# Spreading the finish of the sixth and seventh attention batch over more places of the schedule, with the scatters five places later

## The chip, the cores and the metric

The kernel runs on one core of a Trainium2 chip. The metric is the time of one execution on the device in microseconds (us). The engines are TensorE (PE, with PEld its weight loads), VectorE (DVE), ScalarE (ACT), GpSimd (POOL) and SyncE (SP). SP only issues transfers here. POOL computes and also issues the indirect transfers (gathers and scatters) and the small reads of the routing table. Every engine works off its own list of instructions in order, so an instruction that waits holds up all that stand behind it on its engine.

## What is computed

Block-causal attention over 8 batches (8 heads, 576 positions, head size 64), whose output is the input of a mixture of 8 experts in which every token goes to one expert:

```python
scores = scale * np.matmul(q, k.transpose(0, 1, 3, 2))
scores = np.where(block_i >= block_j, scores, -1e9)     # blocks of 64
attn = softmax(scores); x = (attn @ v)                  # 4608 tokens x 512
logits = x @ w_gate
e_idx = np.argmax(logits, axis=1)                       # the token's expert
gate_w = softmax(logits)[token, e_idx]
eom = 1.0 / (1.0 + np.exp(-(x @ w_output_gate)))
for e in range(8):                                      # tokens of one expert
    h = np.maximum(x[mask] @ w1[e], 0.0)                # 512 -> 1024
    out[mask] = gate_w[mask] * eom[mask, e] * (h @ w2[e])
```

## The kernel before

**Attention runs in 34 positions.** Position p = 0 to 31 does the scores and the softmax of one pair of heads; four positions make a batch, numbered b = 0 to 7 (so batch 5 is the sixth and batch 6 the seventh). The pair's probabilities are transposed one position later and multiplied with v two positions later, so positions 32 and 33 only drain. The order inside a position is the list `PLAN`. Each `|` in it is a *round* (eight per position, r0 to r7), at which every running generator of the list `later` does one step:

```python
PLAN = """
    F0 S1 S0 M1 C0 | | E4- F1 C1 F2 M0 C2 Z0 E1A E1B E0A S2 E0B | F3 F4 C3 V0 Z1 S3 C4 |
    M2 F6 F5 E2A E2B M3 | C5 C6 V1 S4 VM | E3A E3B X M4 | | XM
"""
```

S, M and E are the scores of a row tile (PE), their maximum (DVE, L407 and L411) and the exponentials (ACT, L422); F and C are the transposes of the probabilities (PE, L456) and the copies out of PSUM (L1110); V, VM and X are the products with v. The instruction of L411 (`M4`, the maximum of the last row tile) comes once per position, late in it. It serves below as a clock: *the mark of position p*.

**The finish of a batch** (`finish_steps`) starts at r0 of position 4b+6: the logits of both gates (`logits`, L549), transposed and scaled (`turn_logits`, `scale_logits` L578, `scale_last` L590), summed over the heads (`heads`, L597 and L598), the choice of the expert (`choose`, L601 to L611), ranks in the expert (`ranks`, `own`, `slots`), the gate (`shares`, `gather`, `gate`, `weights`) and the scatter of five row tiles of (token, weight) into the table `tab_d` in DRAM (`scatter`, L658). `T(t)` transposes a row tile of x (PE, L561) and `K(t)` scales it and stores it to `x_d` (DVE, L566). A list with one entry per round says which step comes where. There are three such lists: *pace 1* with 32 entries, *pace 2* with 16 and *pace 3* with 12. Before the change batches 0 to 4 take pace 1, batches 5 and 6 pace 2, batch 7 pace 3. In pace 1 `heads` and two products of `choose` are POOL's, in pace 2 and 3 they are DVE's.

**Loading.** `load_heads` loads a *unit* of four heads (two positions), splits q and k into two fp16 parts on POOL (L105 and L108, eight pieces over eight rounds), turns each half by a DMA transpose (L112, on SP), and copies k's halves across (`swap`, `sw`, L117, DVE).

**The first expert.** `load_first` starts at r0 of position 28: `route_first` takes the counts of batches 0 to 5 (`run_cnt`, column 6) and picks the fullest expert, then its w1 and w2 are loaded. `fetch_ids` (L853) reads table rows, `fetch_x` (L864) gathers rows of x into `xg`; the first three tiles of it may only read the table after the scatters of batches 0 to 5. Eleven rounds later `split_slowly` splits w1 on POOL (L898 and L899, sixteen quarters, one per round, each behind an instruction of ACT), later POOL subtracts for w2 (L894, four chunks). PE needs the gathered x from position 33 on, w1 at the first L1024 (first layer of the experts) and w2 at the first L1053 (second layer).

**The seam.** After batch 7's finish `route_rest` makes a table of steps on DVE; then POOL reads more table rows, gathers x, SP loads the next weights, and the steady loop over the experts' steps begins (L1024 with `xt`, which a DMA transpose delivers).

On POOL, which no hand-written order covers, the scheduler places instructions by the program's order and its own estimate of readiness; on PE, DVE and ACT the written order holds from position 1 on.

Of the kernel before, what the change touches and what calls it, by code (L numbers as in the profile page):

```python
# [11 lines left out]
F32 = mybir.dt.float32  # L12
I32 = mybir.dt.int32
U32 = mybir.dt.uint32
AF = mybir.ActivationFunctionType
ALU = mybir.AluOpType
AX = mybir.AxisListType
PSUM = bass.MemoryType.PSUM
DRAM = bass.MemoryType.DRAM
IOA = bass.IndirectOffsetOnAxis  # L20

P = 128
# [5 lines left out]
def block_attention_top1_moe(  # L28
# [11 lines left out]
    nc = tc.nc  # L40
    B, H, S, D = q.shape
# [466 lines left out]
    def finish_batch(b, sums, xT, pace):  # L508

        for fns in finish_steps(b, sums, xT, pace):  # L510
            for fn in fns:
                fn()
            yield

    def finish_steps(b, sums, xT, pace):
# [13 lines left out]
        se = small.tile([P, NT], F32, name="se")  # L529
        sli = small.tile([P, NT], I32, name="sli")  # L530
        held = {}
        eng = nc.gpsimd if pace == 1 else nc.vector

        def bank():
            return ps_t.tile([P, 512], F32, name="ps_t")
# [90 lines left out]
        def own():  # L626
            nc.vector.tensor_tensor(rk, held["p"][:, 0:NT * E].rearrange("p (t e) -> p t e", e=E), oh, ALU.mult)

        def slots():
            rank = small.tile([P, NT], F32, name="rank")  # L630
            nc.vector.tensor_reduce(rank, rk, AX.X, ALU.add)
            add = small.tile([P, E], F32, name="add")
            nc.vector.tensor_reduce(add, oh.rearrange("p t e -> p e t"), AX.X, ALU.add)
            nc.vector.tensor_tensor(run_cnt[:, b + 1], run_cnt[:, b], add, ALU.add)
            sl = small.tile([P, NT], F32, name="sl")
            nc.vector.scalar_tensor_tensor(sl, er, -float(NTOK), rank, ALU.mult, ALU.add)
            nc.vector.tensor_scalar(sli, sl, float(E * NTOK), None, ALU.add)
# [16 lines left out]
        def scatter():  # L654
            for t in range(NT):
                r = ROWS[t]

                sc = nc.gpsimd.indirect_dma_start(  # L658
                    out=tab_d, out_offset=IOA(ap=sli[0:r, t:t + 1].bitcast(U32), axis=0),
                    in_=idg[0:r, b, t, :], in_offset=None,  # L660
                ).ins
                if scatters:
                    tc.declare_no_dep(sc, group="scatters", reason="distinct slots")
                for ins in tab_init + tab_reads:
                    tc.add_manual_dep(sc, ins.name, SYNC, reason="after earlier accesses of the table")
                tc.add_to_no_dep_group("scatters", sc)
                scatters.append(sc)
# [4 lines left out]
        if pace == 3:  # L672
            return [
                [lge], [ke, lgb], [kb, recips], [turn_logits, turn_last], [scale_logits, scale_last, heads, T(0)], [K(0), choose],
                [ranks], [own, T(1)], [slots, shares, K(1), T(2)], [gather, K(2), gate, T(3)], [weights, scatter, K(3), T(4)], [K(4)],
            ]
        if pace == 2:
            hooks["Z0"] = kb
            hooks["Z1"] = lambda: [fn() for fn in (turn_logits, scale_logits, turn_last, scale_last)]
            return [  # L680
                [lge, lgb], [ke], [recips], [], [heads, T(0)], [K(0), choose], [], [T(1)],
                [K(1), ranks], [own, T(2)], [K(2), slots, shares], [T(3), gather], [K(3), gate], [T(4), weights], [K(4), scatter], [],
            ]
        return [
            [lge], [ke, lgb], [kb, recips], [turn_logits], [scale_logits], [turn_last], [scale_last], [heads],
            [], [], [T(0)], [K(0)], [], [choose], [], [],
            [], [T(1), ranks], [own, K(1), T(2)], [K(2)], [T(3), slots], [shares], [K(3)], [],
            [], [], [T(4)], [K(4)], [gather], [gate], [weights, scatter], [],
        ]

    def counts(col, name):
# [231 lines left out]
    def load_first():  # L923

        route_first()
        fetch_ids(steps[0])
        fetch_ids(steps[1], (0, 1))
        fetch_x(steps[0])
        fetch_x(steps[1], (0, 1))
        with chain():  # L930
            ev = nc.sync.value_load(f_i[0:1, 0:1], min_val=0, max_val=E - 1)

        wc = {}

        def load(w, c):
            dt, nm = ((F16, "hh"), (BF16, "hl"))[c % 2]
            wc[c] = fs.tile([P, KF, 2, P], dt, name=nm).rearrange("p f h n -> p (f h n)").bitcast(F32)
            nc.sync.dma_start(quarter(w, wc[c]), rows_of(w, ev, c))

        for c in range(4):  # L940
            load(w1, c)
        for r in range(11):
            yield
        for c in range(4):
            yield from split_slowly(w1b[0][:, 0, c], w1b[0][:, 1, c].bitcast(BF16), wc[c].rearrange("p (g m) -> p g m", g=KF))
            load(w2, c)
        for r in range(5):
            yield
        for c in range(4):
            with tc.issue_after(last_act[0].ins):  # L950
                split_w2(nc.gpsimd, 0, wc[c], c)
            yield
# [150 lines left out]
    def advance(plan, p, parts, at=()):  # L1103
# [23 lines left out]
        if p > B * NP:  # L1127
            kept.pop("X-", lambda: None)()
        if done:
            later.append(finish_batch(*done, 1 if done[0] < B - 3 else 2 if done[0] < B - 1 else 3))  # L1130
        prods.extend(nxt)

    w1b, w2b, xg = [], [], []
# [163 lines left out]
```

## Time and profile before

| | |
|---|---|
| three timed runs, median | 763.81 us (761.55 to 764.34) |
| the profiled execution's own time | 760.33 us |
| its span, from the first to the last instruction | 758.4 us |
| PE busy | 724.5 us, 96% |
| DVE, ACT, POOL busy | 525.5, 532.1, 341.5 us |
| mark of position 31, the last one with scores | 347.14 us |
| first matmul of the experts' first layer | 360.06 us |

PE is busy almost everywhere, and the changed kernel has the same PE instructions, so what can change is the time in which PE waits or is held back. The granted TensorE clock is 0.998 over the span. Everything that the change moves lies between 100 and 410 us; from there on the loop over the experts is the same.

### The profile page before, as it was taken

Reading aid. Unit: us, or ns where it says so; the run is one execution under the profiler, and the core shown is the slowest. Engines: PE = TensorE matmul, PEld = TensorE weight load, DVE = VectorE, ACT = ScalarE, POOL = GpSimd, SP = SyncE. Lnnn points to the kernel's source line nnn. Section 1 sums busy time; section 2 is a strip of 40 time slices with the busy share of each in tenths; the row PEclk is TensorE's granted clock in tenths of the full one; section 3 lists DMA queues with packets and bytes.
Section 4 is the critical chain, followed back from the end, with each engine's and each line's share of the span. In section 5 each row is a group of like instructions: output and inputs, shape, how many; then the busy total and the mean of one; then the engine's idle time right before and its main releaser. Section 6 shows DMA issues by size and latency. Waiting matters only on the chain.

```text
span 758.4 us, 18741 instructions
## 1 busy us (share of the span) xinstructions
PE 724.5 (96%) x6918; PEld 510.5 (67%) x6918; DVE 525.5 (69%) x1058; ACT 532.1 (70%) x1193; POOL 341.5 (45%) x481
## 2 busy tenths in 40 slices
PE   5899999999999998889998999999999999999996
PEld 3677776767676665666866759667586676686662
DVE  6766776767776779676747958578587685895540
ACT  4999887988888886867117758577576675876531
POOL 6664647474757557396448423232222333301111
PEclk9999999999999999999999999999999999999999
DMA  8899877979696976862167997999999978741611
GB/s 153 175 207 189 178 168 151 203 131 218 123 217 105 214 151 138 198 183 78 64 222 214 290 308 198 290 272 377 294 299 328 302 208 287 222 78 43 240 41 45
DMA packets 256629, 147.87 MB, mean 195 GB/s; under 512 B 224144, under 2 KB 224208, under 8 KB 256528
## 3 DMA queue, kind: packets, MB, share of 16 engines
q1 hardware_dynamic: 248416, 127.30, 67.0%
q0 software_dynamic: 8112, 19.29, 7.8%
q8 instruction: 56, 0.92, 0.6%
q14 instruction: 45, 0.37, 0.2%
HBM read 126.03 MB, written 19.34 MB: 192 GB/s over the span
## 4 chain that ended last, share of the span: by engine, by line
PE 69%; DVE 10%; DMA 7%; ACT 7%; issue 4%; POOL 2%; POOLq 1%; SPq 0%; DVEq 0%; ACTq 0%
PE ps_s L1024 23%; PE ps_t L1053 19%; PE ps_t L456 7%; PE ps_a L491 5%; ACT pt L422 4%; DMA tr<-sp 4%; PE ps_s L390 3%; PE ps_s L391 3%; POOL tab_d L658 2%; PE ps_t L499 1%; PE ps_t L561 1%; ACT pT L1110 1%; DVE nmx L407 1%; PE ps_s L399 1%; PE ps_a L1077 1%
## 5 line engine op out<-in xcount | busy, mean ns | idle before, releaser
L1024 PEld LDWEIGHTS <-w1b 128*128 128x128 f16 (+1 forms) x2208 | 176.1, 98 | 26.1 <-DVE w1b L894 2.7
L1024 PE MATMUL ps_s<-xt,w1b 128*128 128x256 f16 (+5 forms) x1920 | 175.5, 253 | 3.2 <-DMA xt<-xr 1.8
L422 ACT ACTIVATE pt<-ps_s,nbs 128x512 f32<-128x512 f32 (+4 forms) x282 | 155.8, 577 | 25.5 <-DVE nbs L415 24.0
L1053 PE MATMUL ps_t<-w2b,hh 128*128 128x512 f16 (+1 forms) x560 | 166.9, 379 | 0.0
L894 DVE TENSOR_TENSOR w2b<-w2f,w2b 128x1024 bf16<-128x1024 f32 x80 | 92.9, 1220 | 88.8 <-ACT w2b L892 88.8
L407 DVE TENSOR_REDUCE nmx<-ps_s 128x2 f32<-128x1024 f32 (+1 forms) x125 | 102.6, 821 | 45.3 <-PE ps_s L392 44.3
L1110 ACT COPY pT<-ps_t 128x512 f32<-128x512 f32 (+1 forms) x221 | 112.7, 565 | 15.4 <-PE ps_t L456 15.2
L1062 POOL DMA_INDIRECT out_dram<-ys,ids x38 | 48.9, 1288 | 155.2 <-ACT ys L1061 87.7
L456 PE MATMUL ps_t<-ident,pt 128*128 128x128 f32 x768 | 108.5, 277 | 5.2 <-ACT pT L1110 2.9
L1053 PE MATMUL ps_t<-w2b,hl 128*128 128x512 f16 x280 | 106.2, 379 | 0.0
L1061 ACT ACTIVATE ys<-ps_t,ids 128x512 f32<-128x512 f32 (+1 forms) x38 | 26.1, 686 | 113.6 <-PE ps_t L1053 91.5
L1053 PEld LDWEIGHTS <-hh 128*128 128x128 f16 x560 | 54.3, 98 | 61.5 <-issue 0.3
L456 PEld LDWEIGHTS ps_t<-ident,pt 128*128 128x128 f32 x768 | 84.4, 141 | 15.4 <-ACT lgT L555 5.9
L894 DVE TENSOR_TENSOR w1b<-w1f,w1b 128x1024 bf16<-128x1024 f32 x80 | 92.9, 1217 | 1.0 <-ACT w1b L892 0.9
L108 POOL TENSOR_TENSOR sp<-nat,sp 128x320 f16<-128x320 f32 x120 | 89.5, 757 | 8.7 <-DVE sp L105 2.8
L105 POOL CAST sp<-nat 128x320 f16<-128x320 f32 x112 | 49.1, 453 | 82.5 <-ACT pT L1110 77.0
L892 ACT CAST w1b<-w1f 128x1024 f16<-128x1024 f32 x80 | 78.4, 1045 | 3.3 <-DMA w1f<-in_moe_w_dram 3.3
L892 ACT CAST w2b<-w2f 128x1024 f16<-128x1024 f32 x80 | 77.8, 1043 | 1.5 <-DMA w2f<-in_moe_w_dram 1.5
L390 PE MATMUL ps_s<-tr,tr 128*128 128x512 f16 (+1 forms) x250 | 71.8, 303 | 6.5 <-ACT pt L422 6.0
L491 PE MATMUL ps_a<-pT,va 128*64 128x384 f32 (+2 forms) x256 | 74.0, 412 | 0.0
L491 PE MATMUL ps_a<-pT,vb 128*64 128x384 f32 (+2 forms) x256 | 74.0, 412 | 0.0
L391 PE MATMUL ps_s<-sw,tr 128*128 128x512 f16 (+1 forms) x250 | 69.8, 302 | 0.0
(222 smaller groups left out, 1176.0 us busy)
## 6 DMA issues: line engine op xcount, KB each, us to landing
w1f<-in_moe_w_dram SPq DMA_DIRECT2D x80, 512.0 KB
w2f<-in_moe_w_dram SPq DMA_DIRECT2D x80, 512.0 KB
nat<-in_k_dram SPq DMA_DIRECT2D x15, 576.0 KB
nat<-in_q_dram SPq DMA_DIRECT2D x15, 576.0 KB
x_d<-xn SPq DMA_DIRECT2D x32, 256.0 KB
va<-in_v_dram SPq DMA_DIRECT2D x32, 128.0 KB
vb<-in_v_dram SPq DMA_DIRECT2D x32, 128.0 KB
hh<-in_moe_w_dram SPq DMA_DIRECT2D x4, 512.0 KB
```

Of the source, the lines that this page charges most:

```text
L108: last_lo[0] = lo.tensor_tensor(sp[:, sl, 1, :], self.nats[i][:, sl], sp[:, sl, 0, :], ALU.subtract)
L390: nc.tensor.matmul(o, qq, k1[ab][:, 0:n], start=True, stop=False)
L391: nc.tensor.matmul(o, qq, k2[ab][:, 0:n], start=False, stop=False)
L407: nc.vector.tensor_reduce(nmx[t], at[t], AX.X, ALU.max, negate=True)
L422: last_act[0] = nc.scalar.activation(probs[t][:, ab * n:(ab + 1) * n], at[t, ab], AF.Exp, bias=nbs[t][:, ab:ab + 1], scale=SCALE, accum_ou ...
L456: nc.tensor.transpose(held[i][:, P * j:P * j + P], probs[t][:, sl], ident)
L491: nc.tensor.matmul(pa[half, c0:512], vs[a][:, j, :], rows[:, a, j, c0 - P:512 - P], start=(j == 0), stop=(j == 3))
L892: nc.scalar.copy(hi, src)
L894: eng.tensor_tensor(lo[at], src[at], hi[at], ALU.subtract)
L1024: nc.tensor.matmul(ph[:, f4].rearrange("p (h n) -> p h n", n=w), wv[:, cc, f, :], xv[:, cc], start=(k == 0), stop=(k == 3 * KD - 1))
L1053: nc.tensor.matmul(py, hv[:, f, h], wv[:, f, :], start=(k == 0), stop=(k == 3 * KF - 1))
L1110: last_act[0] = nc.scalar.copy(to, of)
```

## The change

Batch 5 now takes pace 1, so that its finish runs over positions 26 to 30 and not over 26 and 27. Pace 2, which only batch 6 still has, grows from 16 to 23 entries: `choose` moves from r5 of its first position to r5 of the second, the ranks, four of the five `T`/`K` and the weights into position 32, and `heads` and the two products go to POOL. In pace 1 the scatter comes five entries later (r3 of the fifth position) and behind the last split instruction issued so far. The counts of a batch (`add`, `run_cnt`) become a step `tally` of their own, ahead of the ranks, since `route_first` at position 28 needs batch 5's. The first expert's table reads and gathers move from r0 of position 28 to r7 of position 30, between two quarters of w1's split.

```diff
-        eng = nc.gpsimd if pace == 1 else nc.vector
+        eng = nc.gpsimd if pace < 3 else nc.vector
...
+        def tally():
+            add = small.tile([P, E], F32, name="add")
+            nc.vector.tensor_reduce(add, oh.rearrange("p t e -> p e t"), AX.X, ALU.add)
+            nc.vector.tensor_tensor(run_cnt[:, b + 1], run_cnt[:, b], add, ALU.add)
+
         def slots():
             rank = small.tile([P, NT], F32, name="rank")
             nc.vector.tensor_reduce(rank, rk, AX.X, ALU.add)
-            add = small.tile([P, E], F32, name="add")
-            nc.vector.tensor_reduce(add, oh.rearrange("p t e -> p e t"), AX.X, ALU.add)
-            nc.vector.tensor_tensor(run_cnt[:, b + 1], run_cnt[:, b], add, ALU.add)
...
-                sc = nc.gpsimd.indirect_dma_start(
+                with tc.issue_after(last_lo[0].ins):
+                    sc = nc.gpsimd.indirect_dma_start(
...
         if pace == 2:
             hooks["Z0"] = kb
             hooks["Z1"] = lambda: [fn() for fn in (turn_logits, scale_logits, turn_last, scale_last)]
             return [
-                [lge, lgb], [ke], [recips], [], [heads, T(0)], [K(0), choose], [], [T(1)],
-                [K(1), ranks], [own, T(2)], [K(2), slots, shares], [T(3), gather], [K(3), gate], [T(4), weights], [K(4), scatter], [],
+                [lge], [ke, lgb], [recips], [], [heads], [T(0)], [K(0)], [],
+                [], [], [], [], [], [choose], [], [tally, T(1)],
+                [ranks, K(1)], [own, T(2)], [K(2), slots, shares], [T(3), gather], [K(3), gate], [T(4), weights], [K(4), scatter], [],
             ]
         return [
             [lge], [ke, lgb], [kb, recips], [turn_logits], [scale_logits], [turn_last], [scale_last], [heads],
-            [], [], [T(0)], [K(0)], [], [choose], [], [],
+            [], [], [T(0)], [K(0)], [], [choose], [], [tally],
             [], [T(1), ranks], [own, K(1), T(2)], [K(2)], [T(3), slots], [shares], [K(3)], [],
-            [], [], [T(4)], [K(4)], [gather], [gate], [weights, scatter], [],
+            [], [], [T(4)], [K(4)], [gather], [gate], [weights], [],
+            [], [], [], [scatter],
         ]
...
         route_first()
-        fetch_ids(steps[0])
-        fetch_ids(steps[1], (0, 1))
-        fetch_x(steps[0])
-        fetch_x(steps[1], (0, 1))
...
             load(w2, c)
+            if c == 2:
+                fetch_ids(steps[0])
+                fetch_ids(steps[1], (0, 1))
+                fetch_x(steps[0])
+                fetch_x(steps[1], (0, 1))
...
-            later.append(finish_batch(*done, 1 if done[0] < B - 3 else 2 if done[0] < B - 1 else 3))
+            later.append(finish_batch(*done, 1 if done[0] < B - 2 else 2 if done[0] < B - 1 else 3))
```

The order of instructions shows three places. First, POOL around batch 0's scatter (positions 9 and 10; `sp` are the split parts of q and k, `tab_d` the table, `lh` and `L` the logits of `heads`). Before:

```order
L108 TENSOR_TENSOR sp<-nat,sp 128x5x64
L658 DMA tab_d<-idg,sli 37120x2 x5
L105 CAST sp<-nat 128x3x64
L105 CAST sp<-nat 128x5x64
L108 TENSOR_TENSOR sp<-nat,sp 128x3x64
L108 TENSOR_TENSOR sp<-nat,sp 128x5x64
L105 CAST sp<-nat 128x5x64 x2
L108 TENSOR_TENSOR sp<-nat,sp 128x5x64 x2
L105 CAST sp<-nat 128x3x64
L108 TENSOR_TENSOR sp<-nat,sp 128x3x64
L597 TENSOR_TENSOR lh<-lh 128x5x64
```

and now:

```order
L108 TENSOR_TENSOR sp<-nat,sp 128x5x64
L105 CAST sp<-nat 128x3x64
L105 CAST sp<-nat 128x5x64
L108 TENSOR_TENSOR sp<-nat,sp 128x3x64
L108 TENSOR_TENSOR sp<-nat,sp 128x5x64
L105 CAST sp<-nat 128x5x64 x2
L108 TENSOR_TENSOR sp<-nat,sp 128x5x64 x2
L105 CAST sp<-nat 128x3x64
L108 TENSOR_TENSOR sp<-nat,sp 128x3x64
L661 DMA tab_d<-idg,sli 37120x2 x5
L597 TENSOR_TENSOR lh<-lh 128x5x64
```

The five scatters have moved from the middle of a unit's split, ahead of the fourth of eight pieces, to behind its last piece and ahead of the next batch's `heads`. The same holds for batches 1 to 4.

Second, DVE at position 26, where batch 5's finish begins. Before, between the marks of positions 25 and 26:

```order
L578 TENSOR_TENSOR lh<-ps_t,rec 128x512
L590 TENSOR_TENSOR lh<-ps_t,rec 64x128
L407 TENSOR_REDUCE nmx_4901<-ps_s 128x2
L415 TENSOR_SCALAR nbs_4906<-nmx_4901 128x1 x2
L407 TENSOR_REDUCE nmx_4902<-ps_s 128x2
L415 TENSOR_SCALAR nbs_4907<-nmx_4902 128x1 x2
L597 TENSOR_TENSOR lh<-lh 128x5x64
L597 TENSOR_TENSOR lh<-lh 128x5x32
L598 TENSOR_TENSOR L<-lh 128x80
L566 TENSOR_TENSOR xn<-ps_t,rec 128x512
L601 TENSOR_REDUCE mx<-L 128x5
```

and now in the same stretch (the last three rows are the mark of position 26 and what follows it):

```order
L407 TENSOR_REDUCE nmx_4896<-ps_s 128x2
L415 TENSOR_SCALAR nbs_4901<-nmx_4896 128x1 x2
L407 TENSOR_REDUCE nmx_4897<-ps_s 128x2
L415 TENSOR_SCALAR nbs_4902<-nmx_4897 128x1 x2
L578 TENSOR_TENSOR lh<-ps_t,rec 128x512
L411 TENSOR_REDUCE nmx_4898<-ps_s 128x1
L415 TENSOR_SCALAR nbs_4903<-nmx_4898 128x1
L590 TENSOR_TENSOR lh<-ps_t,rec 64x128
```

`heads`, the first `K` and the whole of `choose` have left the stretch ahead of the mark, and the scaling of the logits stands behind the maxima of the scores.

Third, POOL in positions 29 to 31 (`hh` and `hl` hold the loaded weights, `w1b` and `w2b` their split, `row` the first row in the table). Before, the table reads and gathers stand right behind batch 5's scatter, ahead of all of w1's quarters:

```order
L658 DMA tab_d<-idg,sli 37120x2 x5
L852 TENSOR_LOAD row_203
L852 ISA x2
L853 ISA
L853 DMA ids<-tab_d 128x2x2
...
L864 DMA xg_5355<-x_d,ids 128x512 x2
L864 DMA xg_5357<-x_d,ids 128x512
L898 CAST w1b_5353<-hh 128x256
L899 TENSOR_TENSOR w1b_5353<-hh,w1b_5353 128x256
```

and now behind its eighth quarter:

```order
L661 DMA tab_d<-idg,sli 37120x2 x4
L903 CAST w1b_5296<-hl 128x256
L904 TENSOR_TENSOR w1b_5296<-hl,w1b_5296 128x256
L858 ISA
L858 DMA ids<-tab_d 128x2x2
L903 CAST w1b_5296<-hh 128x256
L904 TENSOR_TENSOR w1b_5296<-hh,w1b_5296 128x256
L597 TENSOR_TENSOR lh<-lh 128x5x64
...
L858 DMA ids<-tab_d 128x2
L597 TENSOR_TENSOR lh<-lh 128x5x32
L598 TENSOR_TENSOR L<-lh 128x80
L869 DMA xg_5298<-x_d,ids 128x512
```

Batch 6's `heads` stand behind the first table read and around the second, and the gathers lie between later quarters. Further on batch 6's own five scatters, which stood ahead of w2's four chunks, stand behind the second (two), the third (one) and the fourth (two), directly ahead of batch 7's five.

## Rows read from the trace of the kernel before

**Rows 1.** Timeline of DVE, marks: start, us, line, operation, tiles, idle before and releaser.
```profile
48.34 0.76 DVE L411 TENSOR_REDUCE nmx<-ps_s 128x1 f32<-128x576 f32 x1
...
66.45 0.76 DVE L411 TENSOR_REDUCE nmx<-ps_s 128x1 f32<-128x576 f32 x1
...
76.83 0.76 DVE L411 TENSOR_REDUCE nmx<-ps_s 128x1 f32<-128x576 f32 x1 [0.81 <-PE ps_s L399]
...
107.45 0.76 DVE L411 TENSOR_REDUCE nmx<-ps_s 128x1 f32<-128x576 f32 x1
...
117.89 0.76 DVE L411 TENSOR_REDUCE nmx<-ps_s 128x1 f32<-128x576 f32 x1 [0.89 <-PE ps_s L399]
...
160.50 0.76 DVE L411 TENSOR_REDUCE nmx<-ps_s 128x1 f32<-128x576 f32 x1 [0.89 <-PE ps_s L399]
...
243.11 0.76 DVE L411 TENSOR_REDUCE nmx<-ps_s 128x1 f32<-128x576 f32 x1 [0.88 <-PE ps_s L399]
...
274.41 0.76 DVE L411 TENSOR_REDUCE nmx<-ps_s 128x1 f32<-128x576 f32 x1
...
322.06 0.76 DVE L411 TENSOR_REDUCE nmx<-ps_s 128x1 f32<-128x576 f32 x1 [0.97 <-PE ps_s L399]
...
347.14 0.76 DVE L411 TENSOR_REDUCE nmx<-ps_s 128x1 f32<-128x576 f32 x1 [0.38 <-PE ps_s L399]
```

**Rows 2.** Timeline of POOL, position 6: last piece of a split, then heads.
```profile
72.95 0.55 POOL L108 TENSOR_TENSOR sp<-nat,sp 128x192 f16<-128x192 f32 x1
...
78.12 1.47 POOL L597 TENSOR_TENSOR lh<-lh 128x320 f32<-128x320 f32 x2 [4.62 <-DVE lh L590]
...
79.67 0.35 POOL L598 TENSOR_TENSOR L<-lh 128x80 f32<-128x80 f32 x1
```

**Rows 3.** The instructions of L658, the scatter, with its landing times.
```profile
L658 POOL DMA_INDIRECT tab_d<-idg,sli x40: 898/967/1102, 109.0 to 376.0; - x40
...
  issue: 9.4, 31
...
DMA to landing us min/median/max: 3.5/4.3/8.4
```

**Rows 4.** Timeline of DVE: choose, waits for transposes, heads.
```profile
86.48 0.20 DVE L601 TENSOR_REDUCE mx<-L 128x5 f32<-128x40 f32 x1
...
123.87 0.76 DVE L117 COPY sw<-tr 64x2304 f16<-64x2304 f16 x1 [2.41 <-DMA tr<-sp]
...
284.74 2.28 DVE L597 TENSOR_TENSOR lh<-lh 128x320 f32<-128x320 f32 x2
...
308.75 0.76 DVE L117 COPY sw<-tr 64x2304 f16<-64x2304 f16 x1 [2.45 <-DMA tr<-sp]
...
363.00 0.95 DVE L597 TENSOR_TENSOR lh<-lh 128x320 f32<-128x320 f32 x2
```

**Rows 5.** Timeline of PE: a stall, the experts' first matmul, the seam.
```profile
288.21 0.66 PE L456 MATMUL ps_t<-ident,pt 128*128 128x128 f32 x4 [1.34 <-DVE xn L566]
...
360.06 0.28 PE L1024 MATMUL ps_s<-xh,w1b 128*128 128x256 f16 x1
...
408.03 1.03 PE L1024 MATMUL ps_s<-xt,w1b 128*128 128x256 f16 x8 [1.76 <-DMA xt<-xr]
```

**Rows 6.** Timeline of POOL: gather, w1's quarter, w2's chunk, last scatter, next read.
```profile
320.76 1.06 POOL L864 DMA_INDIRECT xg<-x_d,ids  x1 [3.80 <-DMA ids<-tab_d]
...
324.48 0.41 POOL L898 CAST w1b<-hh 128x256 f16<-128x256 f32 x1
...
324.98 0.66 POOL L899 TENSOR_TENSOR w1b<-hh,w1b 128x256 bf16<-128x256 f32 x1
...
353.13 2.56 POOL L894 TENSOR_TENSOR w2b<-hh,w2b 128x256 bf16<-128x256 f32 x4
...
370.88 0.97 POOL L658 DMA_INDIRECT tab_d<-idg,sli  x1 [7.64 <-DVE sli L637]
...
380.56 0.59 POOL L853 DMA_DIRECT2D ids<-tab_d  x1 [3.70 <-DMA tab_d<-idg,sli]
```

More of the change, by code (lines that the diff above doesn't have):

```diff
@@ L656, in scatter @@
                 r = ROWS[t]
-                sc = nc.gpsimd.indirect_dma_start(
-                    out=tab_d, out_offset=IOA(ap=sli[0:r, t:t + 1].bitcast(U32), axis=0),
-                    in_=idg[0:r, b, t, :], in_offset=None,
-                ).ins
+                with tc.issue_after(last_lo[0].ins):
+                    sc = nc.gpsimd.indirect_dma_start(
+                        out=tab_d, out_offset=IOA(ap=sli[0:r, t:t + 1].bitcast(U32), axis=0),
+                        in_=idg[0:r, b, t, :], in_offset=None,
+                    ).ins
                 if scatters:
@@ L674, in finish_steps @@
                 [lge], [ke, lgb], [kb, recips], [turn_logits, turn_last], [scale_logits, scale_last, heads, T(0)], [K(0), choose],
-                [ranks], [own, T(1)], [slots, shares, K(1), T(2)], [gather, K(2), gate, T(3)], [weights, scatter, K(3), T(4)], [K(4)],
+                [ranks], [own, T(1)], [tally, slots, shares, K(1), T(2)], [gather, K(2), gate, T(3)], [weights, scatter, K(3), T(4)], [K(4)],
             ]
```

## The prediction

> **What bounds the kernel now.** I read the page first: PE is busy in nearly every slice up to the middle of the span, and the chain that ended last is mostly PE, with short detours over DVE, POOL, ACT and transfers. So the question is where PE is held back. A single idle gap doesn't tell that well, since engines drift against each other. I therefore took one instruction that comes once per position, the maximum of the last row tile on DVE, and read its start times as marks [rows 1].
>
> Positions 3 to 5 lie before any batch's finish: two positions take 66.45 - 48.34 = 18.11 us. From the mark of position 6 to that of position 10 lies one whole finish in its relaxed form (pace 1) without a scatter in the way: 117.89 - 76.83 = 41.06. The finish thus adds 41.06 - 2 x 18.11 = 4.84 us per batch, mostly PE's own matmuls, which no schedule takes away. Against these two measures the later stretches are too long:
>
> - 117.89 to 160.50, position 10 to 14: 42.61, which is 1.55 above 41.06.
> - 160.50 to 243.11, two cycles: 82.61 against 82.12, 0.49 above.
> - 243.11 to 274.41, position 22 to 25: 31.30 against 107.45 - 76.83 = 30.62, 0.68 above.
> - 274.41 to 322.06, position 25 to 29, batch 5 in pace 2: 47.65, which is 6.59 above.
> - 322.06 to 347.14, position 29 to 31, batch 6 in pace 2: 25.08 against 18.11 + 4.84 = 22.95, 2.13 above.
>
> Together 11.4 us of hold-ups in attention; more than that the change can't return there. What they are is seen on the engines. In positions 25 to 29 PE waits up to 1.34 us for a bank that DVE empties late [rows 5], while DVE is in `heads`, which takes it 2.28 us for two instructions there and 0.95 when it has them to itself [rows 4]. After batch 0's scatter DVE waits 2.41 us for the transposed k of the next unit [rows 4], because the scatter held POOL in the middle of that unit's split. Last, I read the seam: PE reaches the first layer at 360.06 and waits there once, 1.76 us at 408.03, for gathered and transposed x [rows 5].
>
> **The scatters five places later.** Five issues of 0.967 us and 0.30 between them (9.4 us over 31) are 6.3 us of POOL per batch [rows 3]. In position 6, the model of what comes now, POOL ends the last piece of a split at 73.50 and starts `heads` at 78.12, with 4.62 us idle [rows 2]. Put into that gap the scatters push `heads`, which take 1.47 and 0.35, 2 us back, to an end at 82; DVE comes to `choose` at 86.48 [rows 4]. So here the move costs nothing: the cover is 4 us wide, and if it went, each us would hold up DVE and then PE. What it gives is the excess of the first three stretches, 2.72; the 0.49 I can't tie to the scatter and count half: **-2.5** (bounds 0 and -2.7).
>
> **Batch 5 in pace 1.** The excess of 6.59 goes, less what is new. At position 26 POOL now has batch 4's scatter, then the split of the last unit, with `heads` inside it. From the mark of position 26: the last piece ends at -3.3, the scatters at +3.3, four pieces at about 5 us (an estimate from w1's quarter of 0.41 + 0.66, a piece being a quarter longer [rows 6]) reach +8.3, `heads` +10.1. DVE comes to `choose` at 86.48 - 76.83 = +9.65, so it waits 0.5. Late next is the transposed k of the last unit. Before, its copy waits 2.45 us at 308.75 [rows 4], at the place where `route_first`'s small DVE operations stand too; it now hangs on the scatter ahead of the split, so I leave 1.7 of it (bounds 0 and 2.45). **-6.6 + 2.2 = -4.4.** The counts as a step of their own are the same two DVE instructions, five entries ahead of their old place in pace 1; I cost them at nothing, since batch 5's still come a round ahead of `route_first`, and if they came late `route_first` would stand on DVE until they were there.
>
> **Batch 6 in the longer pace 2.** Of the 4.84 about a third (four of five row tiles and the ranks, my split) moves into position 32; PE has it to do there as before, so that is no gain. What can be had is the excess of 2.13. Against it stands POOL's queue, the part that I trust least. From the mark of position 29: batch 0's first scatter stood at 109.0, 1.55 after its mark [rows 3]; five scatters 6.3 and four quarters 4.3 lead to +12.1; the table read waits for the last landing, 3.70 in the row of the last such read [rows 6], so +15.8; then the read 0.6, a quarter 1.1, the second read about 1, `heads` 1.8: +20.3. DVE comes to `choose` about 9.65 after the mark of position 30, less two copies of 0.76 that position 31 doesn't have; with that mark at +11 (10.38 from 66.45 to 76.83, and the first logits are scaled in one go) that is +19.1. So `choose` waits 1.2, and the last maximum and the exponentials behind it too: **-2.1 + 1.2 = -0.9** (bounds -2.1 and +3). `heads` on POOL in place of DVE is otherwise a gift to DVE, which has 2 us less ahead of the mark.
>
> The Trainium skill speaks against such a move: "GPSIMD Engine Reference", section "Elementwise — side-by-side cycle accounting", has a two-input add on GpSimd at 4497 ns against 2293 on VectorE, 1.96 times. Here the pair takes 1.47 on POOL against 0.95 on DVE alone, 1.55 times [rows 2, 4], and 2.28 on DVE beside a busy POOL. By the page, as an estimate, `heads` would take 1.96 x 0.95 = 1.86, end 0.4 later, and the forecast below would be 0.4 higher; I go by the row.
>
> **The tail of POOL's queue.** After +20.3 come three gathers (1.06 and 0.3 each: 4.1) and seven quarters (7.5): w1 is ready at about +32. PE comes to the first layer at 18.11 + 3.2 + 1.2 + 12.92 (360.06 - 347.14) + 1.6 = +37, so w1 has 5 us to spare. Then two products, two w2 chunks of 2.56 [rows 6], two of batch 6's scatters, a chunk, a scatter, a chunk, two scatters: +49.1. Batch 7's scatter started at 370.88 [rows 6], 10.8 after the first layer, which now would be +47.8. So it starts 1.3 late, and with it the table read behind it (at 380.56), the gathers and the transposed x for which PE waited already at 408.03. **+1.3** (bounds 0, if the wait there has other causes, and +4).
>
> **Sum.** -2.5 - 4.4 - 0.9 + 1.3 = -6.5 us. Against the profiled execution's 760.33 that is 753.8. That execution lies 3.5 below the median of the timed runs, 763.81, so the median should be **757.3**. About 0.5%, 3.8 us, is what a measurement of this kernel can tell from no change.
>
> **Rivals.** (1) *Given back at the seam.* Attention ends 7.8 us earlier but the chain through batch 7's scatter, the table read and the gather doesn't follow, because POOL is later than figured: 5 us in place of 1.3 gives 761.0, no change. For it: POOL's load between position 29 and the first layer grows by batch 5's scatters and a landing wait. Against it: before, POOL stood idle 7.64 us ahead of batch 7's scatter [rows 6]. (2) *Slower.* One place decides: the table read at position 30, at which POOL waits for a landing with `heads` and eight quarters behind it. Landings take 3.5 to 8.4 us [rows 3], and the next wait, for the ids, was 3.80 [rows 6]. If POOL is 4.7 later, `choose` waits 6 and the gain falls to 1.8: 762.0, still no change. Slower by over 0.5% needs POOL 10.3 us later than figured, since then all 6.5 are gone and w1 comes late too: 767.6 and more. No row shows two long landings in a row, so this is unlikely. (3) *All hold-ups go*: 11.4 us and no tail, 752.4. For it: POOL may run earlier than I figure, since the scheduler puts batch 5's first scatter ahead of the fourth quarter. Against it: `route_first` and the last unit's transposes still meet at position 28. That the change doesn't do what it says is excluded by the order of instructions.
>
> **Chances.** My forecast, a gain of 3.8 to 9 us: 0.55. Rival 3: 0.13. Rival 1: 0.18. Rival 2 in its mild form, no change: 0.07; in its full form, slower: 0.07. So faster 0.68, same 0.25, slower 0.07. The range that leaves out about 2 in 10 goes from 753.0, near rival 3, to 762.3, which takes in rival 1 and the mild rival 2; the forecast's own is 754.8 to 760.0.
>
> **What would show it.** Marks: position 10 to 14 near 41 (if still 42.6, the scatter wasn't the cause); position 25 to 29 near 43.3; position 29 to the first L1024 about 1 us shorter than 38.0; no wait of DVE for transposes after the scatters except at position 28. On POOL the end of `heads` for batch 6 about 20 us after the mark of position 29, and DVE's wait for it near 1. Batch 7's scatter 12 us after the first L1024, and the wait for x at the seam near 3. I am wrong if that wait grows past 6, if PE waits for w1, or if position 25 to 29 stays above 46.

## The result, and the profile after

The changed kernel takes 769.29 us (median of 6, 767.41 to 771.22), the kernel before beside it 761.37 (6, 760.71 to 764.34): a ratio of 1.0099, interval 1.0080 to 1.0118. It is slower by 1%, 7.9 us; the forecast was 757.3, which is 6.5 below the 763.81 of the first three runs of the kernel before. A second comparison gave 1.0099 again (768.98 against 763.83, 1.0062 to 1.0136). The two traced executions took 760.33 before and 770.35 after.

First the marks of [rows 1], from DVE's timeline of the changed kernel (start, us, engine, line, operation, tiles):

```profile
66.73 0.76 DVE L411 TENSOR_REDUCE nmx<-ps_s 128x1 f32<-128x576 f32 x1
...
118.52 0.76 DVE L411 TENSOR_REDUCE nmx<-ps_s 128x1 f32<-128x576 f32 x1 [0.88 <-PE ps_s L399]
...
160.01 0.76 DVE L411 TENSOR_REDUCE nmx<-ps_s 128x1 f32<-128x576 f32 x1 [0.88 <-PE ps_s L399]
...
274.00 0.76 DVE L411 TENSOR_REDUCE nmx<-ps_s 128x1 f32<-128x576 f32 x1
...
319.14 0.76 DVE L411 TENSOR_REDUCE nmx<-ps_s 128x1 f32<-128x576 f32 x1 [0.53 <-PE ps_s L399]
...
342.14 0.76 DVE L411 TENSOR_REDUCE nmx<-ps_s 128x1 f32<-128x576 f32 x1
```

The mark of position 31 comes 5.0 us earlier than before (342.14, 347.14): so far the change gains, in part because some of batch 6's finish now follows in position 32. Then PE's timeline, its two longest stalls in the stretch that the change moves, and the experts' first matmul:

```profile
299.54 0.17 PE L698 MATMUL ps_t<-run_cnt,ones 128*128 128x8 f16 x1 [2.82 <-DVE run_cnt L632]
...
340.54 0.66 PE L561 MATMUL ps_t<-ident,xT 128*128 128x128 f32 x4
...
342.30 0.18 PE L620 MATMUL ps_a<-run_cnt,ones 128*128 128x40 f16 x1
353.26 1.12 PE L561 MATMUL ps_t<-ident,xT 128*128 128x128 f32 x4 [10.79 <-ACT xT L1116]
...
367.50 0.28 PE L1030 MATMUL ps_s<-xh,w1b 128*128 128x256 f16 x1
```

One wait of 10.79 us, and the first layer starts 7.4 later than before (367.50 against 360.06 in [rows 5]). PE is stopped, but the reader has to walk back over three engines. The releaser is ACT's copy of xT. ACT's and DVE's timelines at that place, ACT first:

```profile
340.38 0.58 ACT L1116 COPY xT<-ps_a 128x512 f32<-128x512 f32 x1
352.87 0.24 ACT L642 ACTIVATE d<-d 128x40 f32<-128x40 f32 x1 [11.91 <-POOL d L611]
353.02 0.19 ACT L1116 COPY xT<-ps_t 128x64 f32<-128x64 f32 x1
...
340.58 0.20 DVE L601 TENSOR_REDUCE mx<-L 128x5 f32<-128x40 f32 x1 [1.51 <-POOL L L598]
...
353.09 0.20 DVE L647 TENSOR_REDUCE zs<-z 128x5 f32<-128x40 f32 x1 [10.20 <-POOL z L610]
```

The second copy of xT waited for nothing of its own: its bank was full at 340.6 (the last L499 of PE). It stands behind the exponential of d (`shares`), DVE's work behind the sum of z, and d and z were on POOL. The Trainium skill says it of all three, "PSUM — Partial Sum Buffer", section "Engine vs sequencer instructions": the queues of ScalarE, VectorE and GpSimd are strictly first in, first out. The trace agrees, with 11.91 us for an operation of 0.24. POOL's timeline shows what stood ahead:

```profile
329.64 0.90 POOL L661 DMA_INDIRECT tab_d<-idg,sli  x1 [0.30 <-issue]
...
336.20 0.77 POOL L858 DMA_DIRECT2D ids<-tab_d  x1 [4.49 <-DMA tab_d<-idg,sli]
...
340.19 0.36 POOL L598 TENSOR_TENSOR L<-lh 128x80 f32<-128x80 f32 x1
341.19 1.09 POOL L869 DMA_INDIRECT xg<-x_d,ids  x1 [0.64 <-issue]
...
351.96 0.67 POOL L904 TENSOR_TENSOR w1b<-hl,w1b 128x256 bf16<-128x256 f32 x1
352.58 0.26 POOL L611 TENSOR_TENSOR d<-L,mx 128x40 f32<-128x40 f32 x1
352.80 0.26 POOL L610 TENSOR_TENSOR z<-L,oh 128x40 f32<-128x40 f32 x1
```

Batch 5's scatters, 4.49 us of landing, the reads, `heads`, three gathers and w1's last seven quarters come first; then two operations of 0.26 us, for which ACT, PE and DVE have been standing since 341 to 343. Last the profile by stretches (busy us of each engine, then PE's granted clock, DMA share, GB/s):

```profile
340.00:350.00 10.00, 1.95 (x35) 1.54 (x31) 2.12 (x8) 0.97 (x3) 8.88 (x16) 0.84 0.30 90
350.00:360.00 10.00, 6.74 (x39) 5.32 (x41) 5.70 (x22) 6.69 (x13) 6.66 (x14) 0.65 0.43 153
353.00:356.00 3.00, 2.74 (x12) 2.38 (x13) 2.74 (x13) 2.89 (x8) 0.28 (x2) 0.50 0.60 208
```

From 343 to 350 only POOL works. After PE's idle time its granted clock is 0.65 over the next stretch, and 0.50 from 353 to 356, which is the lower of its two levels, 1.2 GHz: four transposes of L561 take 1.12 us at 353.26 and took 0.66 at 340.54.

### The profile page after: what moved, and what is told of

It reads as the page before. It is cut to its first block, busy times and chain, and to the rows that moved or that the text cites. A ratio compares the mean times of both kernels' runs of the same rounds, so it can differ in the third digit from the quotient of the medians.

```text
span 768.5 us, 18738 instructions
## 1 busy us (share of the span) xinstructions
PE 728.7 (95%) x6918; PEld 514.2 (67%) x6918; DVE 525.8 (68%) x1048; ACT 534.2 (70%) x1193; POOL 353.5 (46%) x491
## 4 chain that ended last, share of the span: by engine, by line
PE 70%; ACT 8%; DVE 6%; DMA 5%; POOL 5%; issue 4%; POOLq 1%; SPq 0%; DVEq 0%; ACTq 0%
PE ps_s L1030 21%; PE ps_t L1059 18%; PE ps_t L456 8%; PE ps_a L491 6%; ACT pt L422 4%; PE ps_s L390 3%; PE ps_s L391 3%; ACT pT L1116 3%; PE ps_t L561 2%; PE ps_t L499 2%; PE ps_s L399 1%; PE ps_a L490 1%; DMA w1f<-in_moe_w_dram 1%; POOL tab_d L661 1%; PE ps_t L549 1%
## 5 line engine op out<-in xcount | busy, mean ns | idle before, releaser
L1030 PE MATMUL ps_s<-xt,w1b 128*128 128x256 f16 (+5 forms) x1920 | 177.5, 254 | 3.9 <-DVE w1b L899 2.5
L1068 POOL DMA_INDIRECT out_dram<-ys,ids x38 | 53.4, 1406 | 154.5 <-ACT ys L1067 86.6
L456 PE MATMUL ps_t<-ident,pt 128*128 128x128 f32 x768 | 110.9, 281 | 1.0 <-DVE xn L566 0.5
L456 PEld LDWEIGHTS ps_t<-ident,pt 128*128 128x128 f32 x768 | 86.5, 143 | 11.0 <-ACT lgT L555 5.9
```

Source lines behind the costliest of these rows:

```text
L456: nc.tensor.transpose(held[i][:, P * j:P * j + P], probs[t][:, sl], ident)
L1030: nc.tensor.matmul(ph[:, f4].rearrange("p (h n) -> p h n", n=w), wv[:, cc, f, :], xv[:, cc], start=(k == 0), stop=(k == 3 * KD - 1))
```

## The experiments

All are read by the same stretches of marks; "first layer" is the first matmul of xh with w1b (L1024 before). Each median is set against that of the kernel before, run beside it on the same chip. The chips turned out to be of two kinds: on one the kernel before takes 761 to 765 us, on the other 775 to 780. Each chip was used only once (two of the first kind, three of the second, besides the one of the first comparison), so whether the chip itself or its state at that time makes the kind isn't shown.

**1. The products on DVE.** Only batch 6's z and d:

```diff
-            eng.tensor_tensor(z, lz, oh, ALU.mult)
-            eng.tensor_tensor(d, lg, mxb, ALU.subtract)
+            own_eng = nc.gpsimd if pace == 1 else nc.vector
+            own_eng.tensor_tensor(z, lz, oh, ALU.mult)
+            own_eng.tensor_tensor(d, lg, mxb, ALU.subtract)
```

> The changed kernel, but the seventh batch's two small products z and d are made on DVE instead of POOL; its head sums stay on POOL. Theory (the products): PE's 10.8 us of idle time in position 31 come from d and z, which stand on POOL behind two gathers and w1's last quarters; ACT waits for d with the copy of xT behind it, DVE waits for z with the counts behind it, and PE waits for xT. Then the wait falls below 1.5 us, the first layer starts 10 to 12 us earlier than in the changed kernel (near 356), POOL's tail gives about 2 back, and the time is near 760 (758 to 762). Rival (POOL's lateness as such, the table read's wait with everything behind it): PE finds another wait for POOL at the same place, for w1 or at the seam, and the time stays above 766.

767.53 against 765.31, 1.0031 (1.0011 to 1.0052). The wait of 10.79 is gone, so the products made it. But the time stays above 766, as the rival said: PE finds another wait for what POOL does late, behind ACT's casts of w2, which is neither of the rival's two places. ACT, PE and SP's queue of this kernel:

```profile
350.90 1.04 ACT L898 CAST w2b<-hh 128x1024 f16<-128x1024 f32 x1 [4.83 <-DMA hh<-in_moe_w_dram]
...
356.20 1.05 ACT L898 CAST w2b<-hl 128x1024 f16<-128x1024 f32 x1 [3.77 <-DMA hl<-in_moe_w_dram]
...
352.49 1.12 PE L456 MATMUL ps_t<-ident,pt 128*128 128x128 f32 x4 [4.79 <-ACT pT L1117]
...
347.21 0.38 SPq L940 DMA_DIRECT2D hh<-in_moe_w_dram  x1
...
351.68 0.39 SPq L940 DMA_DIRECT2D hl<-in_moe_w_dram  x1
```

w2's chunks are loaded into the buffers from which POOL splits w1. The loads go out at 347.21 and 351.68, when POOL's last quarters of those buffers end (347.19 and 351.66), and ACT's casts stand ahead of PE's copies. So POOL's lateness has two ways to PE, and both had to be closed.

**2. Batch 6 with its old list, all on DVE.** Otherwise the changed kernel.

> The changed kernel with the seventh batch's finish as it was before (old list, all on DVE); the sixth batch in pace 1, the counts apart and the later scatters stay. If the seventh batch's new list is all that loses, the wait of 10.8 us goes, the 2.8 us of PE at the first expert's counts stay, position 25 to 29 stays near 45.1, position 29 to the first layer is 38.0 to 39 as before, and the time is 759 to 761. Rival: the read of the table behind the sixth batch's scatters makes POOL too late for w1 or for the seam whatever the seventh batch does: 764 or more.

766.88, 1.0027 (1.0009 to 1.0045). Position 29 to 31 takes 23.66, then PE waits 2.79 and 3.53 for ACT's copies behind w2's casts: the new list is not all that loses.

**3. The later scatters alone**, on the kernel before: the scatter of batches 0 to 4 five entries later, with its `issue_after`.

> The kernel before with only the scatters of the first five batches five places later. By the prediction's first term 2.5 us less, 759 against 761.4. By the marks of the changed kernel, where the stretch from position 6 to 25 is only 0.4 us shorter than before, no more than 0.5 us less: 761. If the wait for the counts is due to the fifth batch's late scatter alone, it shows here too and the time is 762 to 763.

> The kernel before with only the scatters of the first five batches later, as in the third experiment, on another chip. If its gain of 9 us is the kernel's own, the ratio is 0.986 to 0.992 again; if it is no more than its trace shows against the first trace of before (2.1 us less at the end, 758.4 to 756.3), the ratio is 0.996 to 0.998.

757.03 against 765.31, 0.9881 (0.9864 to 0.9897); on another chip of the same kind 757.87 against 763.83, 0.9925 (0.9899 to 0.9951). This is the part that gains, and more than its term. Where is seen in the table below: position 25 to 29 falls to 44.7. Of the 2.9 us that it loses against the first trace, 2.6 lie between the marks of positions 25 and 26 (16.07 before, 13.48 here). DVE's timeline, the mark of position 26 before, then the head sums of batch 5 (on DVE in both) and that mark in this experiment:

```profile
290.48 0.74 DVE L411 TENSOR_REDUCE nmx<-ps_s 128x1 f32<-128x576 f32 x1
...
282.38 0.84 DVE L597 TENSOR_TENSOR lh<-lh 128x320 f32<-128x320 f32 x2
...
285.52 0.75 DVE L411 TENSOR_REDUCE nmx<-ps_s 128x1 f32<-128x576 f32 x1
```

In [rows 4] the same two started at 284.74 and took 2.28. From there to the mark it was 5.74 us before and is 3.14 now, and that is the 2.6. Then POOL was splitting tiles beside them; now it issues batch 4's scatters. The Trainium skill has the rule, "SBUF — State Buffer", section "Who interferes with whom": a DVE instruction with two SBUF inputs contends with a GpSimd instruction that reads SBUF. The trace agrees, with 2.28 to 0.84.

**4. The scatters back**, otherwise the changed kernel.

> The changed kernel with the scatters of the first six batches back at their old place; all else stays. If the wait for the counts in position 27 (2.8 us) is due to the fifth batch's scatters on POOL ahead of the last split and the sixth batch's head sums, it falls below 1 us. The sixth batch's scatters come some 6 us earlier, so the table read and the products behind it do too: the wait in position 31 falls from 10.8 to about 5, and the time to 762 to 764. If the products' place on POOL alone decides, the wait stays above 9 and the time above 766.

770.15, 1.0058 (1.0040 to 1.0076), a miss. The wait for the counts stays at 2.97, so batch 4's scatters don't make it; the waits of position 31 are 3.36 and 5.35; and position 10 to 25 takes 44.48 + 83.36 + 32.54 = 160.38 instead of the changed kernel's 155.48, a loss that eats what the shorter wait gives. Up to position 25 this kernel differs from the kernel before by the counts alone, and there it takes 3.9 or 2.9 us longer than that (156.5 and 157.4 in the table's two rows).

**5. The table read after w1's last piece, in program order only.**

> The changed kernel with the table read and the gathers of the first experts' rows placed behind w1's last quarters instead of behind its third piece. Theory (POOL's lateness): what makes w1's last quarters late, and behind them w2's loads, ACT's cast of w2 with PE's copies, and the products d and z, is the read that waits 4.5 us for the sixth batch's scatters to land, with 3.3 us of gathers. Then w1 ends near 344 instead of 352.6, the idle time of 10.8 us falls below 2, PE waits some 3 us for gathered x instead, and the time is about 8 us below the changed kernel's, 0.998 of the kernel before. Rival (the sixth batch's five scatters among the quarters and the products' place are enough): the idle time stays above 6 and the time above 1.004.

On a slower chip: 786.08 against 777.79, 1.0118 (1.0054 to 1.0183), PE's wait 10.76. The read still stands on POOL between the same instructions: the scheduler had put it there by its own estimate. It says nothing for or against the theory, only that the changed kernel's wait is there on a slower chip too.

**6. Products on DVE and the read tied behind w1's last quarter.**

```diff
-            if c == 2:
-                fetch_ids(steps[0])
+            if c == 3:
+                with tc.issue_after(piece[0].ins):
+                    fetch_ids(steps[0])
```

`piece` holds the last quarter; the rest as in experiment 1.

> The changed kernel with the products z and d on DVE (as in the first experiment) and the table read tied behind w1's last quarter, which the kernel with the read behind the last piece had not brought about: there it stood on POOL where it stands in the changed kernel. Theory (w1's late quarters hold w2's loads and with them ACT's casts and PE's copies): w1 ends near 343, PE's wait of 4.8 us for ACT's copy behind the cast of w2 falls below 1.5, PE waits 3 to 4 us for gathered x instead, and the first layer starts 3 to 6 us earlier than in the first experiment (358 to 360 instead of 363.35); the ratio is 0.997 to 0.999 where the first experiment had 1.003. Rival (w2's loads are late by themselves, from the queue of transfers): PE's wait behind the cast of w2 stays at 4 to 5 us, and the ratio is 1.003 or more.

763.59 against 763.83, 0.9991 (0.9969 to 1.0013). ACT's casts don't wait any more (342.55 to 347.4 without a gap for transfers), PE waits for gathered x instead:

```profile
351.67 0.94 PE L981 MATMUL ps_t<-ident,xg 128*128 128x128 f32 x4 [1.91 <-DMA xg<-x_d,ids]
...
353.61 1.09 PE L981 MATMUL ps_t<-ident,xg 128*128 128x128 f32 x4 [1.00 <-DMA xg<-x_d,ids]
```

With both ways closed the loss against the kernel before is gone. That against the later scatters alone is not, 757.87 on the same chip: from the mark of position 29 to the first layer it is 43.03 us here and 37.90 there. The first layer came at 360.97, a little later than expected.

**7. The changed kernel and the kernel before again**, on the chip of experiment 6 and of the later scatters' second run.

> The changed kernel, unchanged, beside the others of this call. All theories: the wait of 10 to 11 us in position 31 and that of 2.8 in position 27 again, and a ratio near 1.010 as before.

> The kernel before, unchanged, for a trace on the chip of this call. The profiled execution that the prediction rests on had a span of 758.4 us; the median of the kernel before was 761.4, 765.3 and 777.8 us in three calls. If the marks up to position 25 agree with those of the first trace within 1 us, the later runs are to be read against the first trace; if not, they are read against this one. In the second call's traces PE stood idle 2 to 4 us per batch with no wait named; if that belongs to the chip of that call, it is absent here, and the stretch from position 14 to 22 is 82 to 84 us instead of 85 to 92.

Both came as expected: the waits of the changed kernel are 2.82 and 10.74 again, and the marks of the kernel before agree with those of its first trace within 1 us up to position 25. The stretches on chips of the faster kind, in us, worked out from the marks of each trace (the last from the span):

| | 6-10 | 10-14 | 14-22 | 22-25 | 25-29 | 29-31 | 31 to first layer | to the end |
|---|---|---|---|---|---|---|---|---|
| before | 41.06 | 42.61 | 82.61 | 31.30 | 47.65 | 25.08 | 12.92 | 398.34 |
| before, again | 41.06 | 43.26 | 82.70 | 31.47 | 49.82 | 24.69 | 12.92 | 399.50 |
| changed | 41.43 | 41.49 | 83.09 | 30.90 | 45.14 | 23.00 | 25.36 | 401.00 |
| changed, again | 41.41 | 41.44 | 83.00 | 30.88 | 44.63 | 22.68 | 25.20 | 400.75 |
| seventh batch's old list | 41.41 | 41.43 | 83.72 | 30.88 | 45.46 | 23.66 | 21.86 | 399.05 |
| scatters back | 41.41 | 44.48 | 83.36 | 32.54 | 44.86 | 25.82 | 20.26 | 399.31 |
| products on DVE | 41.42 | 41.45 | 83.03 | 30.88 | 44.63 | 23.19 | 21.99 | 399.05 |
| and read behind w1 | 41.41 | 41.45 | 83.06 | 30.89 | 44.64 | 22.38 | 20.65 | 401.13 |
| later scatters alone | 41.05 | 41.06 | 82.80 | 30.52 | 44.74 | 25.00 | 12.92 | 401.59 |
| the same, again | 41.05 | 41.09 | 82.30 | 30.54 | 44.67 | 24.98 | 12.92 | 401.65 |

Changed again against later scatters again, one chip: 768.98 to 757.87. Position 6 to 25 costs 1.75 us more, 25 to 29 nothing, 29 to the first layer 47.88 - 37.90 = 9.98.

**8. The counts alone, the sixth batch alone, later scatters with the seventh batch's list.** Each is the kernel before with that part; each ran twice, on two slower chips.

> The kernel before with only the counts of the first five batches as a step of their own, five entries earlier (two DVE instructions of 0.21 and 0.17 us). By the prediction they cost nothing. By the marks of the changed kernel, where each second position of a finish takes 9.56 instead of 9.19, they cost 0.3 to 0.4 per batch, 1.5 to 1.9 in all. By the marks of the kernel with the scatters back at their old place, 3.9 us longer from position 10 to 25 than before, they cost 3 to 4: 1.004 to 1.005.

> The kernel before with only the counts of the first five batches as a step of their own. By the marks of the changed kernel against those of the later scatters alone (41.41 to 41.05, 41.44 to 41.09, 83.00 to 82.30, 30.88 to 30.54) the counts cost 0.35 us per batch, 1.7 in all: 1.002. If they also meet the scatters at their old place, as the kernel with the scatters back suggested, position 10 to 14 is 44 to 45 instead of 43 and the ratio is 1.004 to 1.006. By the prediction 1.000.

1.0017 (0.9977 to 1.0057) and 1.0034 (1.0004 to 1.0064): both hold 0.35 us per batch (1.0023), and the first holds a cost of nothing as well. The marks tell more: up to position 25 the kernel with the sixth batch alone, next in order and on the same two chips, differs by these counts alone, and from position 6 to 25 they cost 1.2 and 1.0 us.

> The kernel before with only the sixth batch's finish in pace 1: its counts in a step of their own (the other batches' counts and all scatters at their old places), and the table read behind w1's third piece, since it must follow the sixth batch's scatters. By the prediction's second term 4.4 us less: 0.994. By the runs so far: the hold-up in positions 25 to 29 stays near 45 to 47, since much of it was the fifth batch's scatter; PE waits 2 to 3 us for the counts; and w1's last quarters come so late that the first layer starts 45 us after the mark of position 29 instead of 38: 5 to 8 us more, 1.007 to 1.010.

> The kernel before with only the sixth batch's finish in pace 1 (its counts apart, the table read behind w1's third piece). Theory: the hold-up of positions 25 to 29 falls from 47.7 or 49.8 to near 45, as it does with the later scatters alone, so that the two edits take away the same wait; then w1's last quarters, w2's loads and ACT's casts come late and position 31 to the first layer grows from 12.9 to 17 or more; the ratio is 0.998 to 1.005. Rival (the prediction's term): 0.994, with position 31 to the first layer near 13.

0.9935 (0.9902 to 0.9968) and 0.9888 (0.9805 to 0.9971): a gain there, which the prediction's term (0.994) had and my two expectations had not.

> The kernel before with the later scatters of the first five batches and the seventh batch's longer list, its head sums and products on POOL as in the changed kernel; the sixth batch, its scatters and the table read stay as before. If the products on POOL lose only because the sixth batch's scatters and the table read stand ahead of them, d and z come at most 3 us after DVE's choice, position 29 to 31 takes 23 as in the changed kernel, and the time is that of the later scatters alone or 1 to 2 us less: 0.985 to 0.990. Rival (products behind w1's quarters are late by themselves): PE's idle time in position 31 stays above 6 and the time is 0.996 to 1.0.

> The kernel before with the later scatters and the seventh batch's longer list on POOL, the sixth batch as before. Theory: the products are taken within 1 us of DVE's choice, position 29 to 31 takes 22.5 to 23 and 31 to the first layer 14 to 15.5 instead of 25.0 and 12.9, so that the list moves work and gains nothing: the ratio is that of the later scatters alone, 0.988 to 0.993. Rival (the products on POOL cost wherever they stand): 0.997 or more.

0.9948 (0.9922 to 0.9974) and 0.9917 (0.9881 to 0.9953). The first is above what was expected, the second within it. On POOL d and z wait for DVE, not DVE for them, since w1 was done (first run, POOL):

```profile
356.09 0.67 POOL L909 TENSOR_TENSOR w1b<-hl,w1b 128x256 bf16<-128x256 f32 x1
356.97 0.27 POOL L611 TENSOR_TENSOR d<-L,mx 128x40 f32<-128x40 f32 x1 [0.20 <-DVE mx L601]
358.03 0.26 POOL L610 TENSOR_TENSOR z<-L,oh 128x40 f32<-128x40 f32 x1 [0.79 <-DVE oh L609]
```

**9. Three on one slower chip**, with a trace of the kernel before.

> The kernel before, for the stretches of this chip: position 25 to 29 between 47 and 51, 31 to the first layer 12.9 on a chip of the faster kind (before at 761 to 765) and 18 to 19 on one of the slower kind (778 to 780).

> The sixth batch alone in pace 1. Theory: position 25 to 29 falls to near 45 from the value that the kernel before shows on this chip, 3 to 5 us less; on a chip of the faster kind 4 to 9 us of it are lost again between position 31 and the first layer behind ACT's casts of w2, so that the ratio is 0.998 to 1.006; on one of the slower kind, where the kernel before comes late there by itself, it stays a gain, 0.988 to 0.994 as in the two runs so far. Rival (the prediction's term holds on every chip): 0.994 on either kind.

> The later scatters of the first five batches alone. Position 25 to 29 near 44.7 on a chip of the faster kind, the same value as with the sixth batch alone, and the ratio 0.988 to 0.993. On one of the slower kind the scatters' new place lies where the first five batches' head sums wait, as position 10 to 14 at 46 instead of 43 in the runs with the seventh batch's list showed: then 0.990 to 0.996.

The kernel before took 775.02, the sixth batch alone 772.94, 0.9979 (0.9950 to 1.0007; I had expected 0.988 to 0.994), the later scatters alone 782.94, **1.0114** (1.0073 to 1.0155): on this chip the part that gains on the two faster ones loses, which I had not expected. Stretches:

| | 10-14 | 14-22 | 25-29 | 29-31 | 31 to first layer |
|---|---|---|---|---|---|
| before | 43.01 | 85.44 | 51.18 | 28.44 | 15.91 |
| sixth batch alone | 47.09 | 86.14 | 44.40 | 30.63 | 18.48 |
| later scatters alone | 45.17 | 90.87 | 46.50 | 26.77 | 19.37 |

Either edit takes 25 to 29 down, by 6.8 and 4.7. In this trace the sixth batch loses 4.8 of it again from 29 to the first layer (49.11 against 44.35). But the traced execution took 780.23, 7.3 above its median, with a stall in 10 to 14 that the two traces of experiment 8 don't have (43.00 and 43.11 there, and 43.79 and 40.32 from 29 to the first layer), so its row says little of the median.

The later scatters lose from position 10 to 25: 167.9 us against 159.0 before. That is no matter of this one chip. In experiment 8 the kernels with the scatters at their new and at their old place differ by nothing else up to position 25, and there it is 169.2 against 159.1 on the first chip and 166.1 against 160.1 on the second.

## Why the prediction was wrong

**The step that failed** is in the part on POOL's tail: "Then two products, two w2 chunks of 2.56". Their place was figured well. `heads` ended 21.4 us after the mark of position 29 (forecast 20.3), `choose` waited 1.51 (1.2), w1 was ready at +33.5 (+32). But I priced the products by their own time and did not ask who waits for them. ACT's exponential and DVE's sum do, each in order ahead of what PE needs: 10.8 us for which the sum has no term (its 1.2 is another wait, that of `choose` for `heads`). The prediction's own places held it already: `choose` past its wait at +20.3, the products behind w1 at +32. From the mark of position 29 to the first layer it wanted 1 us less than 38.0, and 48.4 came. Experiment 1 shows that the products are the cause of that wait, and 8 that they are harmless where w1's quarters are done before them. The second thing the sum lacked, w2's loads behind w1's last quarters, is shown by experiments 1 and 6: 1.0099, 1.0031, 0.9991 as the two are closed (the middle one on another chip). The rival that ends slower named the right place, the table read with `heads` and eight quarters behind it, but wanted POOL 10.3 us later than figured; the read waited 4.49 (3.70 figured) and POOL was 1.1 to 1.5 late, but the wait for the products needed no lateness.

**The scatters** (-2.5): the mechanism held. Position 10 to 14 fell to 41.49, and DVE's wait of 2.41 for transposes [rows 4] is gone. (That of 2.45 is gone in the changed kernel too, but not by the scatters: with them alone it is 2.65.) From position 10 to 25 they alone give 2.1 and 3.5 us on chips of the faster kind, the size forecast. What the term left out is position 25 to 29, where 2.9 to 5.1 us of the hold-up were theirs too; in all they give 6.0 and 8.3 there by the medians. That this turns round on slower chips was no case of mine.

**Batch 5** (-4.4): I gave the whole excess of 6.59 to its list. With the scatters moved, its pace 1 adds nothing, 44.63 to 44.67 on one chip: two edits take away one wait. Alone it was tried on slower chips only (0.9935, 0.9888, 0.9979). What it brings is PE's wait of 2.82 for the counts, costed at nothing; `choose` waited for POOL until 296.07, 11.6 after its mark instead of 10.1.

**The counts** as a step: not nothing but 1.75 us over five batches, by marks against the later scatters on one chip, where only they differ up to position 25. In the changed kernel's second trace DVE has them right behind a mark and ahead of the next maximum (88.32 and 88.57, 0.21 and 0.34 us). With the scatters at their old place they cost 2.9 to 3.9 on the faster kind (experiment 4) and 1.0 to 1.2 on the slower (8). The medians can't tell this apart.

**Batch 6** (-0.9): position 29 to 31 took 22.7 to 23.0, as figured; since some of its work then follows in 32, what the list alone gives on the faster kind stays open. On the slower kind it seems to pay: with the later scatters and the list (8) it is 38.17 and 37.67 us from position 29 to the first layer, with the later scatters alone (9) 46.14, though on another chip.

**The seam** (+1.3): PE's wait for x is 1.32, less than the 3 expected; yet the stretch after the first layer is up to 3 us longer, with the later scatters alone too. The seam isn't where it goes: from the first layer to the end of that wait it is 47.98 us before and 47.43 now. The loop behind it takes 350.3 and 351.5 before, 353.5 and 352.7 now, 353.3 and 353.7 with the later scatters alone, at a granted clock of 1.00 before and 0.99 in the others; why wasn't followed.

## What to carry to other kernels

When small operations are moved to a queue with slack, price not their duration but their consumers: who waits in order for them, and what that engine has behind it. POOL's queue was figured to within 1.5 us here, and the time came out 7.9 more instead of 6.5 less. Two edits that are costed from one excess may take away the same wait, so try each alone; and try the better one on more than one chip.

## What the hardware showed unexpectedly

Two kinds of chips. With the same kernel PE waits for "issue" 7.0 us in all before the first layer on the chip of experiment 9, and not once on that of 7. Waits of PE (us in total, times, longest), the kernel before on the slower chip:

```profile
PE ps_t L456 <- issue: 7.0, 7, 1.2
```

They lie beside the scatters (one at 113.81, with POOL issuing them from 109.66 to 115.81). With the later scatters the waits named "issue" are 8.1 us, 1.1 more, too little for the loss of 7.9 there; the granted clock is 0.96 from position 10 to 18, where it was 1.00 before. The cause was not tried.

And a wait of PE can cost twice. In experiment 6 the stretch from 350 to 360 us, in which PE waited 1.91 and 1.00 us after 1.6 idle in the ten before, had a granted clock of 0.66; in the kernel before that stretch has 1.00. Behind the changed kernel's wait of 2.82 us the clock was 0.50. The two stretches, experiment 6 first:

```profile
350.00:360.00 10.00, 7.26 (x59) 4.38 (x63) 2.56 (x4) 1.39 (x3) 9.67 (x16) 0.66 0.32 89
...
299.50:302.00 2.50, 2.46 (x18) 2.40 (x18) 2.15 (x12) 0.72 (x3) 0.16 (x1) 0.50 0.72 135
```
